# Attention and two feed-forward layers on one core: the features' positive part moves to ScalarE, three small operations move to GpSimd, and two buffers and twelve filler transposes change

## The chip, the cores and the metric

The kernel runs on one core of one Trainium2 chip. A core has five engines with a queue each: TensorE (PE in the profile; its weight loads are PEld), VectorE (DVE), ScalarE (ACT), GpSimd (POOL) and SyncE (SP, which here only issues DMAs). The metric is the device time in microseconds of one execution; a kernel's time is the median of its runs.

## The reference, cut to what matters

Three layers follow each other. The first is causal attention with a compressive memory, for 4 batches x 8 heads of 576 rows and 64 features; the second a feed-forward layer with squared ReLU (512 to 2048 to 512, for 2304 tokens); the third a layer of 8 experts of which each token takes one. The change touches the first two.

```python
scores = scale * q @ k.T                      # causal, softmax over keys
local  = softmax(scores) @ v
phi(x) = where(x > 0, x, exp(x) - 1) + 1      # = min(exp(x), 1) + max(x, 0)
mem    = (phi(q) @ M_prev) / (phi(q) @ z_prev + 1e-6)
x      = g * mem + (1 - g) * local            # g = sigmoid(beta), per head
x      = square(relu(x @ w_in)) @ w_out       # w_in, w_out are float64 in the input
x      = gate * relu(x @ w1[e]) @ w2[e]       # e = the best of 8 experts
```

## The kernel before, in words

**Precision.** Each large product is made of three: an operand a is split into a high part (a rounded to a shorter format) and a low part (a minus the high part), and high x high, high x low and low x high are added up in PSUM. So each operand costs a copy (mostly ACT) and a subtraction (DVE or POOL).

**Attention.** Two heads of a batch make a pair; there are 16 pairs, and each pair has 9 units (one for the last 64 rows of both heads, eight for 128 rows of one head). A loop (L627 to L693) takes one unit per step t (144 units, some 160 steps with the run-in and the run-out), and each step issues a bit of many strands: the scores of unit t (`ps`, L485), DVE's masked copy with its row minimum (`A<-ps`, `nm`, L489), ACT's exponential (L495), DVE's sum and reciprocal (`sm`, L503, L504), POOL's scaling (in the first four pairs a diagonal matrix `x_6` of 128x128, L443, afterwards the whole `A`, L446), TensorE's transposes of `A` (`pt`, L451 and L453), ACT's copies of them (`AT`, `ATa`, `ATb`, L641), and the product with the values (`xo`, L586). A page's name x with a line of attention is one of the tiles x_0 to x_8 that later hold the layer's output and until then serve as room.

**The features.** `prep(p)` prepares pair p while pair p-1 is worked on. PE transposes the keys (`tk`) and queries (`tq`); ACT copies them to `hk` and `hq` (L329, L335), DVE makes their low parts; ten DMAs from SP's queue (`moves`, L324) lay them out as `ks`, `qs` and `qz`. Then phi(q): ACT takes e = exp(q) (L355), DVE takes e = min(e, 1) (L359) and e = max(q, 0) + e (L360), POOL multiplies by z (`u`, L364), DVE sums u, adds, and inverts (`nr`, L394 to L398), POOL multiplies e by it (L402), and PE transposes e into `pT`, the memory's operand (L409 to L416). `hq` and `u` share one buffer (tag "hu").

**Conversion.** In the same loop the first half of the 64-bit weights is converted, 16 pieces of 512 columns. A piece has six small steps, and a loop step takes one of them: ACT takes the high words' absolute value (L142); DVE clamps them (L144) and shifts them (L145); DVE merges the sign (L147); DVE merges the low word (L149), which frees the raw buffer for the next DMA; ACT rounds to the high part (L152); POOL subtracts for the low part (L154). The second half is converted later, after attention, in the same way but for its last step.

**The feed-forward layer** begins at loop step 46 (pair 5). Its first chunk's input is split pair by pair by `split_part`: ACT makes `xh` (L733), DVE `xl` (L734). From there on a loop step also holds 12 matmuls of layer 1 (L776) or 6 of layer 2 (L815 to L817).

**What sets the order.** `later(d, engine, f)` puts f into step t + d. Up to step 8 DVE, POOL and SP run in the order of the code, DVE and POOL up to step 71; ACT is free from step 9 on, DVE and POOL from step 72 on. Where an engine is free, a scheduler places its instructions, except that each softmax operation stays behind the instruction recorded before it (`pinned`). PE's order is that of the code throughout. `BUSY` names the early steps at whose start `busy` issues that many transposes of the identity into a PSUM bank that nobody reads (L624).

Of the kernel before, what the change touches and what calls it, by code (L numbers as in the profile page):

```python
# [9 lines left out]
F32 = DT.float32  # L10
F32R = DT.float32r
BF16 = DT.bfloat16
I32 = DT.int32
AF = mybir.ActivationFunctionType
ALU = mybir.AluOpType
# [9 lines left out]
NPP = H // 2  # L25
# [18 lines left out]
W_LEAST = as_float(896 << 20)  # L44
# [12 lines left out]
START, EARLY, MIX = (3, 2, 1), 5, 1  # L57

FREE = 72
STRICT, BUSY = 9, {-5: 14, 0: 12, 2: 6, 4: 4}  # L60


TURN0, TURN1 = 5, 3
# [55 lines left out]
def conversion(nc, st, sh, half, n, lo_eng, w_in, w_out, queue=None, put=nullcontext):  # L119

    V = nc.vector
    raw = st.tile([128, 512, 2], I32, name="raw", tag="raw")
    f = n // 2
    f0 = half * 1024 + f * 128
    queue = queue or nc.sync
    if n % 2 == 0:
        queue.dma_start(raw.rearrange("p (c f) w -> p c (f w)", c=4),
                        w_in[:, f0:f0 + 128].bitcast(I32).rearrange("(c p) f -> p c f", p=128))
    else:
        queue.dma_start(raw.rearrange("p f w -> p (f w)"), w_out[f0:f0 + 128].bitcast(I32))  # L130
    sl = slice((f % 2) * 512, (f % 2) * 512 + 512)
    j = f // 2 + 4 * (n % 2)
    hi, lo = sh.Wh[half][j][:, sl], sh.Wl[half][j][:, sl]
    top, low = raw[:, :, 1], raw[:, :, 0]
    yield
    if half == 0 and n % 4 < 2:
        t = sh.x1[NCH - 4].rearrange("p a b -> p (a b)").bitcast(I32)[:, n % 4 * 512:n % 4 * 512 + 512]
    else:
        t = st.tile([128, 512], I32, name="wt", tag="wt", bufs=WT)
    tf = t.bitcast(F32)  # L140
    with put():
        nc.scalar.activation(tf, top.bitcast(F32), AF.Abs)  # L142
    yield
    V.tensor_scalar(tf, tf, W_LEAST, W_MOST, ALU.max, ALU.min)  # L144
    V.tensor_scalar(t, t, 3, 0x3FFFFFFF, ALU.logical_shift_left, ALU.bitwise_and)  # L145
    yield
    V.scalar_tensor_tensor(t, top, -0x40000000, t, ALU.bitwise_and, ALU.bitwise_or)  # L147
    yield
    V.scalar_tensor_tensor(t, low, 29, t, ALU.logical_shift_right, ALU.bitwise_or)  # L149
    yield  # L150
    with put():
        nc.scalar.copy(hi, tf)  # L152
    yield
    lo_eng.tensor_tensor(lo, tf, hi.bitcast(F32), ALU.subtract)  # L154
    yield
# [36 lines left out]
def attention(tc, sh, q, k, v, M, z, beta, w_in, w_out, mlp, step):  # L192

    nc = tc.nc
    with ExitStack() as ctx:
# [41 lines left out]
        def later(d, eng, f):  # L237
            queue.setdefault((now[0] + d, eng), []).append(f)
# [68 lines left out]
        def prep(p):  # L307
# [5 lines left out]
            if p == 0:  # L313
                hk = qs.rearrange("p a b -> p (a b)")[:, :S]
                hq, lq = ks[:, 0], ks[:, 1]
            else:
                hk = st.tile([128, S], F32R, name="hk", tag="hk", bufs=1)
                hq = st.tile([128, 512], F32R, name="hq", tag="hu", bufs=1)
                lq = st.tile([128, 512], F32R, name="lq", tag="lq", bufs=1)
            qz = new_qz(p) if p else None  # L320
            state[p] = (qs, ks, hq, lq, hk, kl, vn, Mt, qz)
# [30 lines left out]
            u = st.tile([128, 5, 128], F32, name="u", tag="hu", bufs=1)  # L352
            nr = st.tile([128, 10], F32, name="nr", tag="nr")

            later(1, "act", lambda: nc.scalar.activation(e, qn, AF.Exp))  # L355
            yield

            def phi():
                nc.vector.tensor_scalar_min(e, e, 1.0)  # L359
                nc.vector.scalar_tensor_tensor(e, qn, 0.0, e, ALU.max, ALU.add)  # L360

            def weigh():
                later(1, "dve", phi)
                later(1, "pool", lambda: nc.gpsimd.tensor_tensor(u, e, zb.unsqueeze(1).to_broadcast([128, 5, 128]), ALU.mult))  # L364

            if p:
                weigh()
# [332 lines left out]
class Mlp:  # L700
# [23 lines left out]
    def split_part(self, kc):  # L724
# [6 lines left out]
        xl.append(b)  # L731
        x = sh.x1[0][:, kc]
        self.later(2, "act", lambda: nc.scalar.copy(a, x))  # L733
        self.later(2, "dve", lambda: nc.vector.tensor_tensor(b, x, a.bitcast(F32), ALU.subtract))  # L734

    def split_chunk(self, hf, cc):
        if (hf, cc) == (1, NCH - 1):
# [822 lines left out]
```

## Time and profile before

| | us |
|---|---|
| median of 3 runs | 944.61 |
| lowest and highest run | 941.22 and 950.59 |
| the profiled execution's own time | 942.87 |
| its span, from first to last instruction | 941.1 |

| engine | busy us | share of the span |
|---|---|---|
| PE | 898.7 | 95% |
| PEld | 787.7 | 84% |
| DVE | 597.2 | 63% |
| ACT | 524.0 | 56% |
| POOL | 298.4 | 32% |

Read the table as an average over stages: attention alone fills about the first 106 us, attention beside the feed-forward layer the time to about 365 us, then come the rest of the feed-forward layer and the experts. TensorE's granted clock is 0.985 of full speed on average over the span.

### The profile page before, as it was taken

The numbers are of one execution on the slowest core, as the hardware profiler recorded it, in microseconds if no ns is written. First come the engines' busy times: TensorE is split into PE (matmuls) and PEld (weight loads), VectorE is DVE, ScalarE is ACT, GpSimd is POOL, SyncE is SP. The second block draws the span as 40 slices with busy tenths as digits, with TensorE's granted clock in tenths as the row PEclk, the third lists the DMA queues.
The fourth block names the chain that finished last, engine by engine and source line by source line (L and its number), as shares of the span: only waits on it lengthen the run. The fifth ranks groups of instructions, "written<-read, shape, count | busy, mean of one in ns | idle before, by whom it ended". The sixth has DMA issues, their size and how long they took to land.

```text
span 941.1 us, 19239 instructions
## 1 busy us (share of the span) xinstructions
PE 898.7 (95%) x6307; PEld 787.7 (84%) x6307; DVE 597.2 (63%) x1743; ACT 524.0 (56%) x1367; POOL 298.4 (32%) x356
## 2 busy tenths in 40 slices
PE   7978799899999999999999999999999999999993
PEld 5866678788888888898898888888899999999882
DVE  4688977756565653798357778889653535353651
ACT  4677878786676765777555555665322424242540
POOL 5366656744444442000211112442312211111111
PEclk9799999999999999999999999999999999999997
DMA  6666667644444410454201115221061625252521
GB/s 171 144 148 172 177 149 194 159 117 118 110 113 109 103 33 24 137 171 142 92 23 46 46 46 184 76 68 56 24 225 45 208 85 185 86 191 85 184 63 36
DMA packets 107657, 106.86 MB, mean 114 GB/s; under 512 B 66159, under 2 KB 76399, under 8 KB 107520
## 3 DMA queue, kind: packets, MB, share of 16 engines
q1 hardware_dynamic: 101104, 90.17, 34.0%
q0 software_dynamic: 4544, 13.67, 4.5%
q8 instruction: 66, 1.08, 0.5%
q10 hardware_dynamic: 1872, 1.34, 0.5%
q14 instruction: 71, 0.58, 0.2%
HBM read 71.32 MB, written 15.22 MB: 92 GB/s over the span
## 4 chain that ended last, share of the span: by engine, by line
PE 80%; DVE 8%; issue 5%; ACT 2%; DMA 2%; POOL 1%; SPq 0%; ACTq 0%; POOLq 0%; DVEq 0%
PE ps L776 20%; PE psh L1355 11%; PE y L815 7%; PE y L817 7%; PE y L816 7%; PE xo L586 5%; PE ps L485 4%; PE psy L1373 4%; PE psy L1371 4%; PE psy L1372 3%; PE pt L451 3%; DVE A L489 2%; PE pt L453 1%; DVE x L925 1%; PE xo L555 1%
## 5 line engine op out<-in xcount | busy, mean ns | idle before, releaser
L489 DVE CUSTOM_DVE_ANT_0 A<-ps,mask 128x256 f32<-128x256 f32 (+4 forms) x160 | 75.2, 477 | 80.9 <-PE ps L485 79.8
L776 PE MATMUL ps<-xh,Wh 128*128 128x256 f32 x416 | 120.8, 290 | 0.0
L446 POOL TENSOR_SCALAR A<-A,sm,g 128x512 f32<-128x512 f32 (+4 forms) x108 | 86.8, 811 | 102.3 <-DVE sm L504 44.3
L776 PE MATMUL ps<-xl,Wh 128*128 128x256 f32 x416 | 117.6, 283 | 0.0
L776 PE MATMUL ps<-xh,Wl 128*128 128x256 f32 x416 | 117.4, 282 | 0.0
L815 PE MATMUL y<-Wh,gh 128*128 128x512 f32 x288 | 115.6, 402 | 0.0
L817 PE MATMUL y<-Wh,gl 128*128 128x512 f32 x288 | 113.4, 394 | 0.1
L816 PE MATMUL y<-Wl,gh 128*128 128x512 f32 x288 | 113.3, 393 | 0.0
L495 ACT ACTIVATE A<-A,nm 128x576 f32<-128x576 f32 (+2 forms) x144 | 85.0, 590 | 48.4 <-DVE nm L489 21.4
L1357 ACT ACTIVATE hh<-psh 128x512 fp32r<-128x512 f32 x44 | 26.3, 598 | 145.9 <-PE psh L1355 84.8
L780 ACT ACTIVATE r<-ps 128x256 f32<-128x256 f32 x144 | 54.8, 380 | 85.9 <-PE ps L776 77.6
L1355 PE MATMUL psh<-xTh,Wh 128*128 128x256 f32 x352 | 100.0, 284 | 0.9 <-PEq L1363 0.7
L1355 PE MATMUL psh<-xTh,Wl 128*128 128x256 f32 x352 | 99.5, 283 | 0.2 <-DVE Wl L116 0.2
L1355 PE MATMUL psh<-xTl,Wh 128*128 128x256 f32 x352 | 99.3, 282 | 0.0
L786 DVE TENSOR_TENSOR gl<-r,gh 128x256 fp32r<-128x256 f32 x144 | 67.9, 472 | 36.2 <-ACT gh L785 35.8
L1358 DVE SCALAR_TENSOR_TENSOR hl<-psh,hh 128x512 fp32r<-128x512 f32 x44 | 30.4, 690 | 94.0 <-ACTq L1345 38.1
L776 PEld LDWEIGHTS ps<-xh,Wh 128*128 128x128 f32 x416 | 79.1, 190 | 3.9 <-issue 0.4
L776 PEld LDWEIGHTS ps<-xl,Wh 128*128 128x128 f32 x416 | 79.2, 190 | 2.8 <-issue 0.2
L776 PEld LDWEIGHTS ps<-xh,Wl 128*128 128x128 f32 x416 | 79.3, 191 | 0.0
L785 ACT CAST gh<-r 128x256 fp32r<-128x256 f32 x144 | 58.6, 407 | 34.6 <-PE y L816 31.9
L1355 PEld LDWEIGHTS psh<-xTh,Wh 128*128 128x128 f32 x352 | 66.9, 190 | 2.5 <-ACTq L1345 1.1
L1355 PEld LDWEIGHTS psh<-xTl,Wh 128*128 128x128 f32 x352 | 66.8, 190 | 0.8
(349 smaller groups left out, 2414.6 us busy)
## 6 DMA issues: line engine op xcount, KB each, us to landing
x<-in_moe_w_dram SPq DMA_DIRECT2D x48, 512.0 KB, 4.1
ks<-hk SPq DMA_DIRECT2D x60, 128.0 KB, 3.3
raw<-in_moe_w_in_dram SPq DMA_DIRECT2D x15, 512.0 KB, 3.8
raw<-in_moe_w_out_dram SPq DMA_DIRECT2D x15, 512.0 KB, 4.2
x2p<-x SPq DMA_DIRECT2D x18, 256.0 KB, 2.3
x2d<-x SPq DMA_DIRECT2D x18, 256.0 KB, 2.0
vn<-in_v_dram SPq DMA_DIRECT2D x32, 128.0 KB, 2.8
part<-x2p SPq DMA_DIRECT2D x16, 256.0 KB, 3.0
```

The costliest lines, as they stand in the source:

```text
L446: nc.gpsimd.tensor_scalar(A, A, a, b, ALU.mult, ALU.mult)
L489: nc.vector.tensor_tensor_reduce(A[:, a:a + w], tiles[j][:, :w], mask[:, end - w:end], -1.0, 3e38, ALU.add, ALU.min, nm[:, j:j + 1])
L495: nc.scalar.activation(A[:, :n], A[:, :n], AF.Exp, bias=nm[:, 0:1], scale=-1.0, accum_out=sm[:, i:i + 1])
L586: nc.tensor.matmul(x[hs, cols], vn[:, kb, hs], mov, start=h is None and kb == 0, stop=h is not None and end and kb == last)
L776: nc.tensor.matmul(ps[:, :CH], a, b, start=n == 0, stop=n == len(ops) - 1)
L780: self.later(1, "act", lambda: nc.scalar.activation(r, ps[:, :CH], AF.Relu))
L785: self.later(3, "act", lambda: nc.scalar.copy(gh, r))
L786: self.later(3, "dve", lambda: nc.vector.tensor_tensor(gl, r, gh.bitcast(F32), ALU.subtract))
L815: nc.tensor.matmul(y, gh[:, sl], wh, start=first, stop=False)
L816: nc.tensor.matmul(y, gh[:, sl], wl, start=False, stop=False)
L817: nc.tensor.matmul(y, gl[:, sl], wh, start=False, stop=last)
L1355: nc.tensor.matmul(ps[:, a], w[kc][:, sl], x[:, kc], start=kc + j == 0, stop=kc + j == 5)
```

## The change

Six edits. (1) `BUSY` gets two more steps: 8 filler transposes at step 5 and 4 at step 6. (2) The clamp of the conversion (L144) goes to POOL for the first half of the weights, in a step of its own; the shift that shared its step goes to the next one, beside the sign's merge, so a piece has as many steps as before. (3) `hq` of pairs 1 to 6 gets a buffer of its own, in the ring of two that the feed-forward layer uses for its output `x2`; from pair 7 on it shares "hu" with `u` as before. (4) ACT takes u = max(q, 0) behind e = exp(q), and DVE makes e = min(e, 1) + u in one instruction in place of two. (5) z's product, which overwrites u, comes one loop step later from pair 3 on. (6) `xl` of the first chunk goes from DVE to POOL.

```diff
-STRICT, BUSY = 9, {-5: 14, 0: 12, 2: 6, 4: 4}
+STRICT, BUSY = 9, {-5: 14, 0: 12, 2: 6, 4: 4, 5: 8, 6: 4}
...
     with put():
         nc.scalar.activation(tf, top.bitcast(F32), AF.Abs)
     yield
-    V.tensor_scalar(tf, tf, W_LEAST, W_MOST, ALU.max, ALU.min)
+    (nc.gpsimd if half == 0 else V).tensor_scalar(tf, tf, W_LEAST, W_MOST, ALU.max, ALU.min)
+    yield
     V.tensor_scalar(t, t, 3, 0x3FFFFFFF, ALU.logical_shift_left, ALU.bitwise_and)
-    yield
     V.scalar_tensor_tensor(t, top, -0x40000000, t, ALU.bitwise_and, ALU.bitwise_or)
...
                 hk = st.tile([128, S], F32R, name="hk", tag="hk", bufs=1)
-                hq = st.tile([128, 512], F32R, name="hq", tag="hu", bufs=1)
+                if p < NPP + 3:
+                    hq = mlp.st.tile([128, 512], F32R, name="hq", tag="x2")
+                else:
+                    hq = st.tile([128, 512], F32R, name="hq", tag="hu", bufs=1)
...
-            later(1, "act", lambda: nc.scalar.activation(e, qn, AF.Exp))
+            def grow():
+                nc.scalar.activation(e, qn, AF.Exp)
+                nc.scalar.activation(u, qn, AF.Relu)
+
+            later(1, "act", grow)
             yield
 
             def phi():
-                nc.vector.tensor_scalar_min(e, e, 1.0)
-                nc.vector.scalar_tensor_tensor(e, qn, 0.0, e, ALU.max, ALU.add)
+                nc.vector.scalar_tensor_tensor(e, e, 1.0, u, ALU.min, ALU.add)
 
             def weigh():
                 later(1, "dve", phi)
-                later(1, "pool", lambda: nc.gpsimd.tensor_tensor(u, e, zb.unsqueeze(1).to_broadcast([128, 5, 128]), ALU.mult))
+                later(2 if p > 2 else 1, "pool", lambda: nc.gpsimd.tensor_tensor(u, e, zb.unsqueeze(1).to_broadcast([128, 5, 128]), ALU.mult))
...
         x = sh.x1[0][:, kc]
         self.later(2, "act", lambda: nc.scalar.copy(a, x))
-        self.later(2, "dve", lambda: nc.vector.tensor_tensor(b, x, a.bitcast(F32), ALU.subtract))
+        self.later(2, "pool", lambda: nc.gpsimd.tensor_tensor(b, x, a.bitcast(F32), ALU.subtract))
```

Line numbers of the changed kernel are larger by 1 to 6 behind the edits (L364 is L370 there, L443 is L449, L485 is L491, L624 is L630).

How the instructions stand on three engines, before and with the change. First PE at loop steps 5 and 6 (`w` is the fillers' bank, `tp` the transposed features, `pt` the transposed softmax); before:

```order
L485 MATMUL ps<-kl,ks 128x256
L485 MATMUL ps<-qs,ks 128x384 x2
L485 MATMUL ps<-kl,ks 128x384
L409 MATMUL tp<-ident,e 128x128 x4
L453 MATMUL pt<-x_6_96,A_144 128x128 x4
L453 MATMUL pt_377<-x_6_96,A_144 128x128
L453 MATMUL pt<-x_6_96,A 128x128 x4
```

With the change:

```order
L491 MATMUL ps<-kl,ks 128x256
L630 MATMUL w<-ident 128x128 x8
L491 MATMUL ps<-qs,ks 128x384 x2
L491 MATMUL ps<-kl,ks 128x384
L415 MATMUL tp<-ident,e 128x128 x4
L459 MATMUL pt<-x_6_96,A_144 128x128 x4
L459 MATMUL pt_386<-x_6_96,A_144 128x128
L630 MATMUL w<-ident 128x128 x4
L459 MATMUL pt<-x_6_96,A 128x128 x4
```

Two rows of fillers came in; the rest of PE's order, to the program's end, is the same.

Second, POOL in pair 1 (L364, with the change L370, is z's product for pair 2; L144 is a clamp, L154 a conversion's last step); before:

```order
L402 TENSOR_TENSOR e<-e,nr 128x640
L443 TENSOR_SCALAR x_6_96<-ident,sm,g_186 128x128 x4
L364 TENSOR_TENSOR u<-e,zb 128x640
L443 TENSOR_SCALAR x_6_96<-ident,sm,g_186 128x128 x2
L154 TENSOR_TENSOR Wl_0_79<-x_5_95,Wh_0_71 128x512
```

With the change:

```order
L408 TENSOR_TENSOR e<-e,nr 128x640
L144 TENSOR_SCALAR x_5_95<-x_5_95 128x512
L449 TENSOR_SCALAR x_6_96<-ident,sm,g_186 128x128 x4
L370 TENSOR_TENSOR u<-e,zb 128x640
L144 TENSOR_SCALAR x_5_95<-x_5_95 128x512
L449 TENSOR_SCALAR x_6_96<-ident,sm,g_186 128x128 x2
L154 TENSOR_TENSOR Wl_0_79<-x_5_95,Wh_0_71 128x512
```

Two clamps came in, one of them between z's product and the next two scalings. In the following pairs an `xl` (L740) comes in as well, behind two scalings.

Third, ACT in pair 4, where the features of pair 5 are made (`AT` are the transposed softmax of the last 64 rows); before:

```order
L355 ACTIVATE e<-qn 128x640
L495 ACTIVATE A,sm<-A,nm 128x128
L142 ACTIVATE wt<-raw 128x512
L641 COPY AT<-pt 128x512
L641 COPY AT_1435<-pt_1433 128x128
L495 ACTIVATE A,sm<-A,nm 128x384
```

With the change:

```order
L359 ACTIVATE e<-qn 128x640
L501 ACTIVATE A,sm<-A,nm 128x128
L360 ACTIVATE u<-qn 128x640
L142 ACTIVATE wt<-raw 128x512
L647 COPY AT<-pt 128x512
L647 COPY AT_1450<-pt_1448 128x128
L501 ACTIVATE A,sm<-A,nm 128x384
```

The positive part (L360) came in ahead of the high words' absolute value and of the copies that TensorE waits for; in other pairs the scheduler puts it elsewhere in the same stretch.

## Rows read from the trace of the kernel before

**Rows 1.** Two stretches: busy us (instructions) of PE, PEld, DVE, ACT, POOL, clock, DMA, GB/s.

```profile
40.00:190.00 150.00, 130.72 (x1051) 107.82 (x1052) 123.29 (x371) 119.16 (x343) 93.40 (x99) 0.99 0.67 168
190.00:370.00 180.00, 180.00 (x1420) 155.56 (x1419) 103.98 (x380) 124.88 (x377) 75.41 (x88) 1.00 0.39 93
```

**Rows 2.** TensorE's waits between 34 and 190 us, first and last of 15.

```profile
PE ps L485 <- DVE nm L489: 4.0, 5, 1.3
...
PE pt L451 <- DVE kl L330: 0.2, 1, 0.2
```

**Rows 3.** Short stretches, columns as in the first group.

```profile
15.20:21.30 6.10, 2.87 (x18) 2.19 (x18) 3.87 (x17) 3.83 (x13) 2.75 (x6) 1.00 0.73 235
22.90:33.00 10.10, 10.10 (x60) 8.63 (x58) 4.83 (x20) 4.47 (x15) 3.04 (x3) 0.50 0.75 168
...
91.00:99.30 8.30, 4.87 (x30) 3.44 (x30) 7.52 (x24) 8.22 (x24) 4.59 (x6) 1.00 0.55 158
177.80:183.50 5.70, 2.64 (x18) 2.04 (x18) 5.70 (x20) 3.71 (x11) 3.59 (x3) 0.97 0.53 119
183.50:186.70 3.20, 3.20 (x14) 3.01 (x15) 1.22 (x4) 1.65 (x5) 3.09 (x6) 0.52 0.76 170
```

**Rows 4.** TensorE in order of time: start, us, instruction [idle before and releaser].

```profile
10.52 0.88 PE L624 MATMUL w<-ident 128*128 128x128 f32 x6
...
16.54 0.61 PE L485 MATMUL ps<-qs,ks 64*128 64x384 f32 x2 [1.38 <-DVE nm L489]
...
20.33 0.49 PE L453 MATMUL pt<-x,A 128*128 128x128 f32 x2 [1.38 <-ACT AT L641]
21.26 1.13 PE L453 MATMUL pt<-x,A 128*128 128x128 f32 x8 [0.45 <-POOL x L443]
```

**Rows 5.** DVE's groups by form up to 380 us: busy us, mean ns, idle before.

```profile
L359 DVE TENSOR_SCALAR e<-e 128x640 f32<-128x640 f32 x16 | 8.7, 544 | 2.4 <-ACT e L355 2.4
L144 DVE TENSOR_SCALAR x<-x 128x512 f32<-128x512 f32 x8 | 4.1, 509 | 1.4 <-ACT x L142 1.3
L144 DVE TENSOR_SCALAR wt<-wt 128x512 f32<-128x512 f32 x8 | 3.3, 412 | 0.0
L734 DVE TENSOR_TENSOR xl<-x,xh 128x256 fp32r<-128x256 f32 x4 | 1.8, 440 | 0.0
```

**Rows 6.** All engines in order of time, pair 2's features.

```profile
45.36 0.82 DVE L360 SCALAR_TENSOR_TENSOR e<-qn,e 128x640 f32<-128x640 f32 x1
...
45.40 0.60 SPq L324 DMA_DIRECT2D qz<-hq  x1
...
48.09 1.55 POOL L364 TENSOR_TENSOR u<-e,zb 128x640 f32<-128x640 f32 x1 [5.53 <-DVE sm L503]
...
48.13 2.06 DVE L147 SCALAR_TENSOR_TENSOR x<-raw,x 128x512 int32<-128x512 int32 x1
...
50.57 0.94 PE L453 MATMUL pt<-x,A 128*128 128x128 f32 x6 [1.33 <-POOL x L443]
```

**Rows 7.** POOL's groups by form: busy us, mean ns, idle before.

```profile
L446 POOL TENSOR_SCALAR A<-A,sm,g 128x512 f32<-128x512 f32 x24 | 24.7, 1038 | 27.4 <-ACT pT L410 12.9 <-DVE sm L504 10.7 <-ACT ATb L641 2.5
...
L754 POOL TENSOR_TENSOR xl<-x,xh 128x256 fp32r<-128x256 f32 x16 | 12.0, 778 | 57.2 <-ACT xh L753 57.2
```

**Rows 8.** ACT's exponential of the queries, by form: busy us, mean ns, idle before.

```profile
L355 ACT ACTIVATE e<-qn 128x640 f32<-128x640 f32 x14 | 10.5, 752 | 0.0
```

**Rows 9.** TensorE in order of time, pair 4.

```profile
96.85 1.12 PE L555 MATMUL xo<-pT,Mt 128*128 128x512 f32 x2 [1.36 <-ACT pT L416]
...
99.22 0.63 PE L451 MATMUL pt<-ident,A 128*128 128x128 f32 x4 [0.48 <-ACT AT L641]
```

**Rows 10.** All engines in order of time, pair 8's features.

```profile
168.12 0.60 SPq L324 DMA_DIRECT2D qz<-hq  x1
...
171.49 0.68 ACT L142 ACTIVATE wt<-raw 128x512 f32<-128x512 f32 x1
...
172.69 1.96 POOL L364 TENSOR_TENSOR u<-e,zb 128x640 f32<-128x640 f32 x1 [0.96 <-DMA kn<-in_k_dram]
```

## The prediction, made before the changed kernel ran

> **What bounds the kernel now.** I read the busy time by stretch first, then TensorE's waits, then the clock. From 190 us on TensorE is the bound without a gap: it is busy 180.00 of 180 us while ACT is busy 124.88, DVE 103.98 and POOL 75.41 [rows 1]. All six edits lie in attention and in the conversion beside it, that is before about 365 us, so behind 190 us they can cost only what TensorE's full queue does not cover. What is left to win lies before 190 us. From 40 to 190 us TensorE is busy 130.72 of 150 us and idles 19.3, while DVE is busy 123.29 and ACT 119.16 [rows 1]: the three form a ring (scores, row minimum, exponential, transposes, copies, scores again), and none is full all the time. Who ends TensorE's waits there is told by 15 rows that come to 19.4 us, of which the first and the last stand here [rows 2]: ACT ends nine of them, 10.9 us, DVE four, 6.0, POOL two, 2.5.
>
> The second thing to see is the clock. Between 22.9 and 33.0 us the granted clock is 0.50, that is 1.2 GHz in place of 2.4, and TensorE is busy all 10.10 us while ACT is busy 4.47 and DVE 4.83 [rows 3]: here TensorE alone is the bound, and only since it is slow. In the 6.1 us before the fall it was busy 2.87, with gaps of 1.38, 1.38 and 0.45 us [rows 3, 4]. A second fall, to 0.52 over 3.2 us from 183.5, follows a stretch with 2.64 of 5.7 us busy; a stretch with 4.87 of 8.3 us busy (91.0 to 99.3) is followed by none [rows 3].
>
> **The change, part by part.** The sum is made against the profiled execution, 942.87 us, which is 1.7 below the median of 944.61 and inside the 941.22 to 950.59 of the runs.
>
> *Fillers.* Six of them took 0.88 us [rows 4], so eight take about 1.2 and four 0.6. Eight stand in front of the scores that came after the gap of 1.38 and four in front of the transposes that came after the gap of 0.45; the second gap of 1.38 stays open. In the first gap they cost nothing, in the gap of 0.45 at most 0.15; I take 0.1. They raise the busy time before the fall from 2.87 to about 4.5 of 6.1 us (1.2 and 0.4 more), 73%, above the 59% (4.87 of 8.3) after which the clock held. So I take it that the clock holds. Then TensorE's work of 10.1 us needs 5.05, and ACT's 4.47 plus a positive part of 0.75 [rows 8], 5.2, is the next bound: at most 4.9 us are won, at least none (it falls all the same). Since ACT reached only 79% in the ring (119.16 of 150), 5.2 becomes 6.6, and I take 3.5.
>
> *DVE's relief.* Gone from DVE before 190 us are nine of the sixteen min instructions (9 x 0.544 = 4.9), the sixteen clamps (4.1 + 3.3) and four `xl` (1.8) [rows 5], together 14.1 us. The surviving instruction of phi has the form of the one that stays today, two tensors in, and I keep its 0.82 [rows 6]. The shift, moved one step back, no longer stands ahead of the next row minimum. What can arrive at once is what DVE ends of TensorE's waits, 6.0; the lower bound is nothing, where ACT's turn stands right behind. I take half, 3.0, since ACT ends nearly twice as much as DVE. Behind 190 us the rest of the min instructions is worth nothing.
>
> *The buffer.* In pair 2 DVE had finished phi at 46.2, but POOL's product began at 48.09, when the DMA of `qz` from `hq`, issued at 45.40, had landed: u and hq are one buffer [rows 6]. Behind the product stood the scalings, and TensorE waited 1.33 us for one. With a buffer of its own, hq no longer holds u, the product can run at 46.2, and that wait goes. Bounds: nothing, or POOL's whole 2.5; I take 1.3. The ring of `x2` that lends the buffer is not in use by the feed-forward layer until its first chunk is done, by which time hq has only pair 6 left there; I cost that at nothing. Were it not so, a query copy on ACT would stand behind the landing of an `x2` store. On SP two issues of raw weights change places with one of the moves, at no cost.
>
> *POOL's load.* Nearest rows: a two-step operation on 128x512 took 1.038 on POOL, a subtraction of 128x256 0.778 [rows 7]. Sixteen clamps and four `xl` are 16.6 + 3.1 = 19.7 us more on POOL, which idles 56.6 of the 150 us [rows 1]. A clamp makes a new wait: DVE's shift, and all of DVE's order behind it up to step 71, needs it a step later. A step before pair 5 lasts about 2 us (the feed-forward layer begins at step 46, at 106 us), and where z's product and a clamp fall into one step they take 2.6; so the shift may be late by 0.6, once in each of pairs 1 to 8, 4.8 at most, nothing where the product starts earlier as above. I take 0.5.
>
> One thing weighs against this part. In pair 2 DVE's sign merge, of 512 columns, lasted 2.06 us, from the start of POOL's product to 0.55 us behind its end; the phi instruction of the same form, of 640 columns, had taken 0.82 [rows 6]. So about 1.2 us of DVE were lost beside one product of 1.55. The Trainium skill (SBUF — State Buffer, section "SBUF: two separate sides") says that VectorE and GpSimd take a shared pair of ports as an exclusive lock for a whole instruction, where VectorE reads two tensors from SBUF or runs in a two-port mode; by it a clamp on GpSimd is no free move, and this term would be up to 5.6 slower in place of 3.0 faster; the row agrees as far as one pair can. By the row alone, POOL's new 19.7 us cost DVE between nothing and 19.7; DVE is rid of 14.1, so the sum of both lies between -14.1 and +5.6. I take the relief as above, and the other end is a rival.
>
> *ACT's load.* The positive part reads and writes what the exponential does, 0.75 us [rows 8]. In pair 4 ACT is the bound: busy 8.22 of 8.30 us [rows 3], and TensorE waits 1.36 for `pT` and 0.48 for `AT` [rows 9]; with the change the positive part stands ahead of `AT`. If it arrives in full in each of pairs 2 to 6 it costs 3.8, if nowhere nothing; I take two of the five, 1.5. At the very start it stands ahead of the casts that the first scores need, 0.75 late, against 0.54 that DVE saves there: I take 0.3. Behind 190 us TensorE's queue covers it; without that cover seven pairs would cost 5.3.
>
> Sum: 942.87 + 0.1 - 3.5 - 3.0 - 1.3 + 0.5 + 1.5 + 0.3 = 937.5 us, 0.8% below the median.
>
> **The rivals.** *Forecast* (0.50): as above, 932 to 941.
>
> *DVE is master everywhere* (0.18): ACT's exponentials are late only since the row minima are. Then DVE's 6.0, POOL's 2.5 and the clock's 4.9 arrive in full, the second fall goes as well (half of 3.2, 1.6), and the positive part hides: 942.87 - 15.0 = 928, range 924 to 932. For it: DVE busy 5.70 of 5.70 us before the second fall [rows 3]. Against it: pair 4 [rows 9].
>
> *The clock falls all the same* (0.18), since one gap of 1.38 stays and the positive part adds a delay before it: 937.5 + 3.5 = 941, range 938 to 944.
>
> *POOL takes back what DVE gave* (0.08). Each of POOL's new instructions holds DVE up for its length, as the product did with the sign merge. The place is the conversion, where the clamp runs while DVE merges another piece, and the end is DVE's net +5.6 in the ring in place of -3.0: 937.5 + 8.6 = 946, slower than before. It decides from the point where DVE loses more than 14.1 us to POOL. Beside it stands the lock of the Trainium skill's page named above, which would give this result if every one of them met such an instruction. Against it: many of DVE's instructions here read one tensor from PSUM and a mask, and the product that held DVE longest moves ahead.
>
> *ACT waits for a DMA* (0.06). From pair 7 on the positive part writes the buffer that hq's DMAs still read. In pair 8 the last one was issued at 168.12 and the product that waited for it began at 172.69; ACT's place for the positive part is behind the instruction that ends at 172.17 [rows 10]. So ACT would stand 0.5 us and then work 0.75, and all copies out of PSUM with it. Nine pairs x 1.25 = 11 us, if TensorE's queue covers none of it: 937.5 + 11 = 948.5. Against it: ACT is busy 124.88 of 180 us [rows 1].
>
> **How the numbers follow.** The prediction is the forecast's 937.5. The range leaves out the slow two rivals (0.14) and the low tail of the fast one: 928 to 945. The forecast's own range is 932 to 941. What a measurement of this kernel can tell from no change is about 1%: 935.2 to 954.1 around 944.61. Faster by more: the fast rival (0.18) and, of the forecast, the part below 935.2 (0.22), 0.40. Slower by more: the upper tails of the last two and what I have not thought of, 0.06. Within: 0.54.
>
> **What would show it.** Clock 1.00 from 15 to 40 us, and the scores of pair 1 some 3 us earlier; if the clock falls at a later place before 60 us, the first term failed. The product of pair 2 within 1 us of phi, and no wait of TensorE for the scaling behind it. Clamps on POOL of about 1 us, DVE's shift without a wait for them. TensorE's waits between 34 and 190 us: DVE's near 3, ACT's unchanged or larger, with `AT` of pair 4 later against the scores by up to 0.75. Wrong I would be if DVE's mean times of the merges rise by more than their sixteen clamps saved, or if TensorE idles behind 190 us.

## The result, and the profile after

The changed kernel takes 954.34 us (median of 6 runs, 953.09 to 957.32), the kernel before, run beside it, 945.32 (941.22 to 950.59). The ratio is 1.0114, with an interval of 1.0083 to 1.0145: slower, by 9.0 us between these medians and by 10.8 by the ratio, where 937.5 (928 to 945) was forecast. The profiled execution of the changed kernel took 953.85 us, its span is 952.1.

The windows of the changed kernel answer to [rows 1, 3]; the columns are the same.

```profile
22.90:33.00 10.10, 9.77 (x85) 8.08 (x84) 6.21 (x26) 7.96 (x24) 4.39 (x6) 1.00 0.73 166
40.00:190.00 150.00, 127.50 (x1007) 103.80 (x1006) 105.87 (x311) 114.56 (x324) 113.87 (x107) 0.97 0.65 157
190.00:370.00 180.00, 177.17 (x1365) 153.00 (x1365) 105.81 (x385) 128.79 (x381) 74.06 (x93) 0.98 0.41 98
190.00:200.00 10.00, 7.17 (x33) 6.16 (x34) 6.96 (x25) 5.69 (x15) 5.84 (x8) 0.66 0.58 128
```

The clock now holds from 22.9 to 33 us (1.00, before 0.50). But from 40 to 190 us VectorE (DVE) is busy 17.4 us less than before and TensorE 3.2 less: what VectorE was relieved of turned into idle time, not into speed. GpSimd (POOL) is busy 20.5 us more. And the stretch from 190 us, full before, has a hole: 7.17 of 10 us at a clock of 0.66.

Where the time goes is told by the first scores of each pair (the first matmul of 128x320 into `ps` from `qbh`). Their starts, against the kernel before (30.21 us in pair 1, 104.83 in pair 5, 156.33 in pair 7, 202.96 in pair 9); behind pair 9's first scores the difference stays as it is. Each row is one profiled execution beside one of the kernel before, so 2 or 3 us in a place can be chance (clamp_back stands at +3.01 in pair 9, and its ratio is 1.0000); the medians are from different chips, so small differences go by the ratios, each to the kernel before run beside it:

```
kernel (median us; ratio to before, 95%)            pair 1  pair 5  pair 7  pair 9
the change (954.3; 1.0083 to 1.0145)                 -2.10   +1.42   +5.36  +11.30
clamp_back (944.6; 0.9980 to 1.0019)                 -2.42   -1.44   -0.64   +3.01
clamp_alone (958.6; 1.0102 to 1.0179)                +0.10   +7.18  +11.92  +16.23
relu_undone (956.7; 1.0099 to 1.0168)                -2.96   +2.22   +6.22  +10.38
fillers_alone (940.9; 0.9953 to 0.9995)              -3.13   -3.20   -1.67   -3.07
clamp_and_relu_undone (940.1; 0.9956 to 0.9996)      -3.09   -2.40   -2.57   -3.99
fillers_and_relu (952.7; 1.0065 to 1.0126)           -2.79   +5.81   +7.44  +10.36
multiply_for_clamp (943.2; 0.9976 to 1.0015)         -2.14   -1.51   -2.59   +1.04
shift_behind (952.5; 1.0059 to 1.0138)               -2.63   -0.87   +2.91   +9.64
load_only (943.8; 0.9999 to 1.0035)                  -2.89   -2.75   -1.79   -0.22
relu_to_pair_6 (943.0; 0.9977 to 1.0009)             -2.12   -2.73   -0.48   -1.50
vector_less (935.3; 0.9890 to 0.9936)                -3.14   -3.22   -5.80   -9.11
clamp_earlier (945.4; 1.0000 to 1.0044)              -2.64   -0.56   -1.99   +1.77
bunch_alone (944.2; 0.9979 to 1.0030)                -2.39   +0.19   -0.52   +3.42
best_candidate (942.5; 0.9964 to 0.9999)             -3.46   -0.39   -1.71   -0.87
behind_and_earlier (947.3; 1.0037 to 1.0071)         -2.58   -3.30   -3.16   +2.13
behind_xl_on_vector (953.5; 1.0097 to 1.0130)        -2.61   +0.03   +1.93   +9.15
subtract_load (946.7; 1.0017 to 1.0061)              -2.51   -1.75   +1.03   +2.06
```

GpSimd's groups by form, from 15 to 215 us of the changed kernel (busy us, mean ns), beside [rows 7]; L144 is the clamp, L452 the multiplication that was L446:

```profile
L144 POOL TENSOR_SCALAR x<-x 128x512 f32<-128x512 f32 x8 | 15.4, 1919 | 0.2 <-ACT x L142 0.2
L144 POOL TENSOR_SCALAR wt<-wt 128x512 f32<-128x512 f32 x8 | 15.3, 1914 | 0.0
...
L452 POOL TENSOR_SCALAR A<-A,sm,g 128x512 f32<-128x512 f32 x10 | 10.1, 1020 | 7.0 <-DVE sm L510 6.9
```

A clamp takes 1.92 us, not the 1.04 that the prediction took from the multiplication of the same shape. VectorE's waits from 20 to 205 us (total us, times, longest):

```profile
DVE wt L146 <- POOL wt L144: 6.7, 4, 2.4
DVE e L366 <- ACT u L360: 5.4, 4, 2.5
DVE x L146 <- POOL x L144: 4.2, 5, 1.1
```

The shift (L146) waits 10.9 us for clamps, phi (L366) 5.4 for the Relu. How one such wait reaches TensorE stands in the order of time, pair 8:

```profile
186.91 1.91 POOL L144 TENSOR_SCALAR wt<-wt 128x512 f32<-128x512 f32 x1
...
188.79 1.26 POOL L154 TENSOR_TENSOR Wl<-wt,Wh 128x512 fp32r<-128x512 f32 x1
188.85 1.48 DVE L146 TENSOR_SCALAR wt<-wt 128x512 int32<-128x512 int32 x1 [2.37 <-POOL wt L144]
...
190.33 0.48 DVE L495 CUSTOM_DVE_ANT_0 A<-ps,mask 128x320 f32<-128x320 f32 x1
...
190.87 0.61 PE L491 MATMUL ps<-ks,qs 128*128 128x512 f32 x1 [2.77 <-DVE nm L495]
```

VectorE stands 2.37 us for the clamp. Then its shift lasts 1.48 us beside GpSimd's next subtraction, which started 0.06 us before it. That is so throughout: of the changed kernel's 16 shifts, the twelve beside a scaling of one tensor on GpSimd took 0.41 to 0.48 us; the four that began beside an instruction with two tensors took 0.91 to 1.50, and each ended 0.28 us after that instruction. The row minimum comes behind wait and shift, TensorE waits 2.77 us for it, and its clock falls (the window at 190 us).

### The profile page after: what moved, and what is told of

Read it like the earlier page. It is cut to its first block, busy times and chain, and to the rows that moved or that the text cites. A ratio compares the mean times of both kernels' runs of the same rounds, so it can differ in the third digit from the quotient of the medians.

```text
span 952.1 us, 19216 instructions
## 1 busy us (share of the span) xinstructions
PE 901.7 (95%) x6319; PEld 787.9 (83%) x6319; DVE 585.3 (61%) x1707; ACT 533.8 (56%) x1383; POOL 323.8 (34%) x376
## 4 chain that ended last, share of the span: by engine, by line
PE 74%; DVE 10%; issue 6%; POOL 5%; ACT 2%; DMA 2%; SPq 0%; ACTq 0%; POOLq 0%; DVEq 0%
PE ps L782 19%; PE psh L1361 11%; PE y L821 7%; PE y L823 6%; PE y L822 6%; PE xo L592 4%; PE psy L1379 3%; PE psy L1377 3%; PE ps L491 3%; PE psy L1378 3%; PE pt L457 3%; DVE A L495 2%; DVE x L931 1%; POOL wt L144 1%; POOL x L144 1%
## 5 line engine op out<-in xcount | busy, mean ns | idle before, releaser
L452 POOL TENSOR_SCALAR A<-A,sm,g 128x512 f32<-128x512 f32 (+4 forms) x108 | 78.2, 732 | 87.8 <-DVE sm L510 31.2
L1377 PE MATMUL psy<-Wh,hh 128*128 128x512 f32 x168 | 67.0, 399 | 0.1
```

The source lines that it names most:

```text
L452: nc.gpsimd.tensor_scalar(A, A, a, b, ALU.mult, ALU.mult)
L1377: nc.tensor.matmul(y[h], xh, wh, start=g + a == 0, stop=False)
```

## The experiments

Theory W was that the loss is the wait: a slow clamp ahead of VectorE's shift, with the softmax's minima behind the shift. Theory R was that ScalarE's (ACT's) Relu costs it. Others came up on the way. (Two operations move to GpSimd, the clamp and `xl`, and one tile, `hq`, gets another buffer; the title counts more.)

**clamp_back, clamp_alone, relu_undone, fillers_alone: which part?** The first is the change with the clamp as before:

```diff
-    (nc.gpsimd if half == 0 else V).tensor_scalar(tf, tf, W_LEAST, W_MOST, ALU.max, ALU.min)
-    yield
+    V.tensor_scalar(tf, tf, W_LEAST, W_MOST, ALU.max, ALU.min)
     V.tensor_scalar(t, t, 3, 0x3FFFFFFF, ALU.logical_shift_left, ALU.bitwise_and)
+    yield
```

> The changed kernel with one part undone: the clamp is VectorE's again, in one step with its shift as before; the other five edits stay. Theory W (the wait: a clamp of 1.91 us on GpSimd, 16 of them, stands ahead of VectorE's shift, and all that lies behind the shift in VectorE's order is late): the 10.9 us of waits of the shift go, the scores of pairs 1 to 9 come earlier by 10 to 13 us in all, 941 to 944 us. Theory R (ScalarE's Relu: 16 x 0.74 us more on ScalarE, and phi waits 5.4 us for it): the loss stays, 950 to 954 us.

clamp_alone is the opposite diff on the kernel before.

> The kernel before with one part of the change done: the clamp of the first weights' conversion on GpSimd in a step of its own, the shift a step later. Theory W: 952 to 958 us (945.3 and the 10 us that pairs 5 to 8 lost, and falls of the clock that differ from place to place). Theory R: 944 to 947 us, as the kernel before.

relu_undone:

```diff
-                nc.scalar.activation(u, qn, AF.Relu)
...
-                nc.vector.scalar_tensor_tensor(e, e, 1.0, u, ALU.min, ALU.add)
+                nc.vector.tensor_scalar_min(e, e, 1.0)
+                nc.vector.scalar_tensor_tensor(e, qn, 0.0, e, ALU.max, ALU.add)
```

> The changed kernel with the Relu undone: VectorE computes phi in two instructions, ScalarE only the exponential. Theory W: 951 to 955 us, since the wait of phi for ScalarE (9.3 us in 9 waits) lies mostly beside the wait of the shift. Theory R: 943 to 947 us.

fillers_alone is the kernel before with `5: 8, 6: 4` in `BUSY`.

> The kernel before with the added fillers alone (two entries of the table BUSY). If the fillers keep the clock up through pair 0 and nothing takes it back: granted clock 1.00 from 22.9 to 33 us, the scores of pair 1 some 3 us earlier and the whole at 941 to 943 us. The rival, that the 3 us are given back in pair 1 where the clock falls after the next gap (in the changed kernel it was 0.83 from 40 to 50 us): 944 to 946 us.

Measured: 944.6, 958.6, 956.7 and 940.9 us. The clamp makes the loss (the first three lie 0.6, 0.6 and 1.7 us above theory W's ranges, and far from theory R's): without it the rest of the change is at the kernel before, alone it costs 1.4% (1.0 to 1.8), and undoing the Relu gives nothing back while the clamp is there. The fillers hold the clock, and nothing takes the 3 us back (fillers_alone's window):

```profile
22.90:33.00 10.10, 9.62 (x88) 8.24 (x87) 7.41 (x30) 7.56 (x24) 4.86 (x7) 1.00 0.70 159
```

**clamp_and_relu_undone, fillers_and_relu, relu_to_pair_6: what the Relu costs.** The first joins the diffs of clamp_back and relu_undone.

> The changed kernel without its clamp on GpSimd and without its Relu: what is left is the fillers, hq's buffer, the later product of z and the low part xl on GpSimd. The fillers alone gave 940.9, the change with the clamp undone 944.6. If the Relu is what costs these 3.7 us (phi waits for it 7.3 us in 4 waits with the clamp undone): 939 to 942 us. If hq's buffer, the product or xl cost them: 943 to 946 us.

The second is fillers_alone with the Relu and the one instruction of phi, but hq still in u's buffer:

```diff
-            later(1, "act", lambda: nc.scalar.activation(e, qn, AF.Exp))
+            later(1, "act", grow)
...
```

> The kernel before with two parts of the change: the fillers and the Relu. If the Relu costs the 3.7 us: 943.5 to 946 us, with the loss in pairs 7 and 8 (the scores of pair 9 against the kernel before at +2 to +3 us, where the fillers alone stood at -3.1). If not: 940 to 942 us.

The third is clamp_back with the Relu only where hq has a buffer of its own:

```diff
+                if p < NPP + 3:
+                    nc.scalar.activation(u, qn, AF.Relu)
...
```

> The changed kernel with the clamp back on VectorE, and ScalarE's Relu in pairs 0 to 6 alone, where hq has the buffer that it doesn't share with u; pairs 7 to 15 have phi in VectorE's two instructions again. Theory S (the Relu waits, on ScalarE, for hq to leave the buffer that it shares with u from pair 7 on; with the clamp back pairs 7 and 8 lost 3.65 us against the kernel before): pair 9's scores at -0.5 us or earlier against the kernel before instead of +3.0, 940 to 942 us. Theory R (16 x 0.74 us more on ScalarE is what costs): 942.5 to 945 us.

Measured: 940.1, 952.7 and 943.0 us. The second came out far beyond what I had expected: with a shared buffer the Relu has to stand behind hq's transfers, and so late in ScalarE's order (its own waits for them are 1.3 us in two), and phi on VectorE waits for it, 28.2 us in nine waits:

```profile
DVE e L363 <- ACT u L357: 28.2, 9, 6.6
```

So, by these waits, hq's own buffer is what makes the Relu affordable (the product's later step and `xl` on GpSimd, which this run lacks as well, were not tried one by one). From pair 7 on, where the change goes back to the shared one, the same wait of phi returns. In clamp_back the Relu stands 3.9 us behind the exponential in pair 7, and in pair 8 it waits for a transfer:

```profile
144.21 0.78 ACT L359 ACTIVATE e<-qn 128x640 f32<-128x640 f32 x1
...
148.07 0.73 ACT L360 ACTIVATE u<-qn 128x640 f32<-128x640 f32 x1
...
148.91 0.82 DVE L366 SCALAR_TENSOR_TENSOR e<-e,u 128x640 f32<-128x640 f32 x1 [1.92 <-ACT u L360]
...
173.44 0.74 ACT L360 ACTIVATE u<-qn 128x640 f32<-128x640 f32 x1 [0.88 <-DMA kn<-in_k_dram]
...
174.28 0.82 DVE L366 SCALAR_TENSOR_TENSOR e<-e,u 128x640 f32<-128x640 f32 x1 [3.78 <-ACT u L360]
```

and phi waits for it 1.92 us in pair 7 and 3.78 in pair 8. Without the Relu from pair 7 on (relu_to_pair_6) VectorE has no such wait from 135 to 205 us, and pair 9 stands at -1.50 in place of +3.01. In the whole time that is 944.6 against 943.0 (ratios 1.0000 and 0.9993), within the spread of either, so the place is shown and the size is not; 943.0 itself lies where theory R had it. A second part is the start: the first scores come at 8.30 us in clamp_and_relu_undone, at 9.05 in clamp_back, 9.34 in relu_to_pair_6.

**multiply_for_clamp and clamp_forms: what the price hangs on.** The clamp is left out; other operations stand at its place on GpSimd (for the first half of the weights). In multiply_for_clamp:

```diff
+        nc.gpsimd.tensor_scalar(tf, tf, 1.0, 1.0, ALU.mult, ALU.mult)
```

> The changed kernel with the first weights' clamp left out: in its place GpSimd multiplies the same tile in place twice by 1.0, so order, steps, waits and shapes are the changed kernel's. If the price of 1.91 us belongs to the maximum and minimum: about 1.04 us each, as the softmax's multiplication of 128x512; by theory W the waits of the shift then fall from 10.9 us to under 5 and the time to 945 to 949 us. If it belongs to the place (in place, the tile, the company of VectorE's shifts): 1.9 us each and 953 to 956 us.

In clamp_forms, by the piece's number n:

```diff
+    elif n % 4 == 0:
+        nc.gpsimd.tensor_scalar(tf, tf, W_LEAST, None, ALU.max)
+    elif n % 4 == 1:
+        nc.gpsimd.tensor_scalar(tf, tf, W_LEAST, 1.0, ALU.max, ALU.mult)
+    elif n % 4 == 2:
+        nc.gpsimd.tensor_scalar(tf, tf, 1.0, 0.0, ALU.mult, ALU.add)
+    else:
+        nc.gpsimd.tensor_scalar(tf, tf, 1.0, W_MOST, ALU.mult, ALU.min)
```

> The changed kernel with four other operations at the clamp's place on GpSimd, in turn by n modulo 4, each leaving out a part of the clamp: the maximum alone, maximum then a multiplication by 1, a multiplication and an addition, a multiplication and the minimum. Max and min together took 1.91 us, two multiplications 0.62 us. If each of maximum and minimum has the high price by itself: about 1.0 to 1.3 us for the maximum alone and for the mixed pairs, 0.62 us for multiplication and addition. If one of them already brings a slow routine: 1.9 us wherever one stands.

The rows of GpSimd by form, of multiply_for_clamp (one of its two) and then of clamp_forms (L147 maximum alone, L149 maximum and multiplication, L151 multiplication and addition, L153 multiplication and minimum):

```profile
L145 POOL TENSOR_SCALAR wt<-wt 128x512 f32<-128x512 f32 x8 | 4.9, 615 | 0.0
```

```profile
L153 POOL TENSOR_SCALAR wt<-wt 128x512 f32<-128x512 f32 x4 | 7.7, 1935 | 0.3
L149 POOL TENSOR_SCALAR x<-x 128x512 f32<-128x512 f32 x4 | 7.7, 1928 | 0.2 <-ACT x L142 0.2
L147 POOL TENSOR_SCALAR x<-x 128x512 f32<-128x512 f32 x4 | 6.0, 1501 | 0.0
...
L151 POOL TENSOR_SCALAR wt<-wt 128x512 f32<-128x512 f32 x4 | 2.5, 620 | 0.0
```

The price is the operation's, and neither expectation had it whole: 0.62 us for multiplications and additions by constants, 1.50 for one maximum, 1.93 for any pair with a maximum or minimum in it. With 0.62 us in the clamp's place, and the order of instructions on TensorE, VectorE, ScalarE and GpSimd that of the change, the shift's waits are 2.4 us in place of 10.9 and the time is 943.2 (from 20 to 205 us):

```profile
DVE wt L149 <- POOL wt L145: 2.4, 3, 1.1
```

The length of the clamp alone makes the 11 us. clamp_forms, run once, took 950.5. The Trainium skill (GPSIMD Engine Reference, section "Engine selection") says that with one input GpSimd runs roughly at line rate; that fits 0.62 us beside VectorE's 0.41 to 0.51 [rows 5], and not the 1.92 of maximum and minimum, and the measurement decides.

**load_only, shift_behind, clamp_earlier: wait or load?** load_only is clamp_back with GpSimd's work and no wait; the order on the other engines is clamp_back's:

```diff
+        spare = sh.Wl[0][7][:, 512:1024]
...
+        nc.gpsimd.tensor_scalar(spare, spare.bitcast(F32), W_LEAST, W_MOST, ALU.max, ALU.min)
```

> The changed kernel with the clamp back on VectorE and, at the place of each of the 16 clamps on GpSimd, the same maximum and minimum of 128x512 on a tile that nothing waits for. So GpSimd carries the changed kernel's load (16 x 1.9 us), and VectorE's shift waits for nothing there. Against 944.6 us with the clamp back and 954.3 us of the change: theory W (the wait of the shift does the harm) 944 to 947 us; theory L (GpSimd's load does it: scalings and low parts behind the clamp in GpSimd's order are late) 951 to 957 us.

shift_behind is the change with the shift and its merge one step later:

```diff
     yield
+    yield
     V.tensor_scalar(t, t, 3, 0x3FFFFFFF, ALU.logical_shift_left, ALU.bitwise_and)
     V.scalar_tensor_tensor(t, top, -0x40000000, t, ALU.bitwise_and, ALU.bitwise_or)
-    yield
```

> The changed kernel with the shift and its merge one step later, together with the second merge, so that VectorE does a row minimum or more of the softmax between the clamp's start and the shift; the number of steps is unchanged. Theory W (the wait does the harm): the shift's waits fall from 10.9 us to under 4, 945 to 949 us. Theory L (GpSimd's load does the harm: 30.7 us more, under which low parts, scalings and VectorE's own instructions get late or longer): 952 to 956 us.

clamp_earlier:

```diff
+    half or nc.gpsimd.tensor_scalar(tf, tf, W_LEAST, W_MOST, ALU.max, ALU.min)
     yield
-    (nc.gpsimd if half == 0 else V).tensor_scalar(tf, tf, W_LEAST, W_MOST, ALU.max, ALU.min)
+    half and V.tensor_scalar(tf, tf, W_LEAST, W_MOST, ALU.max, ALU.min)
     yield
```

> The changed kernel with GpSimd's clamp issued one step earlier, in the step of its absolute value; VectorE's order stays the changed kernel's (two small swaps apart), GpSimd's load too. Theory W (the wait of the shift and what lies behind it in VectorE's order): the shift's waits fall from 10.9 us to under 4 and the time to 944 to 948 us. Theory C (whatever comes of a conversion that has a clamp of 1.9 us in it: the chain of one conversion is longer, its later steps late, VectorE's merges beside other GpSimd work): 950 to 955 us, as with the shift behind (952.5), whose waits were gone as well.

load_only carries more than the change's load,

```profile
L149 POOL TENSOR_SCALAR Wl<-Wl 128x512 fp32r<-128x512 f32 x16 | 33.2, 2076 | 0.1
```

and takes 943.8 us: 33 us more on GpSimd cost nothing that can be measured (ratio 1.0017, 0.9999 to 1.0035; clamp_back 1.0000). Theory L, that GpSimd's load does the harm, falls for maximum and minimum. clamp_earlier takes 945.4; the shift's waits are 4.0 us (2.5 and 1.5):

```profile
DVE wt L146 <- POOL wt L142: 2.5, 3, 1.3
...
DVE x L146 <- POOL x L142: 1.5, 2, 1.1
```

That is theory W, and gives back about 9 of the 10 to 11 us. But shift_behind stayed at 952.5, where theory L had it, with only 1.6 us of waits. Three runs looked into it.

**bunch_alone, behind_and_earlier, behind_xl_on_vector.** All have the step structure of shift_behind. bunch_alone has its clamp on VectorE (`V.tensor_scalar` in the clamp's line).

> The control of the run with the shift one step later: shift and both merges in one step as there, but the clamp on VectorE, in the step that it had on GpSimd. If the bunch of three instructions (2.0 to 2.9 us in a row on VectorE, row minima behind it) did the harm there: 949 to 953 us. If not: 943 to 946 us, as the run with the clamp back (944.6).

behind_and_earlier has clamp_earlier's diff as well.

> The kernel with the shift one step later, its clamps on GpSimd one step earlier: VectorE's order is that of the shift behind (952.5 us), but the clamp is over a whole step before the shift begins. If the slow clamp does harm there by ending just as the shift begins, where GpSimd's next subtraction starts at the same moment and holds the shift (one shift of 2.69 us was seen there): 943 to 947 us. If the bunch of shift and merges beside GpSimd's load does it: 950 to 954 us.

behind_xl_on_vector undoes `xl`:

```diff
-        self.later(2, "pool", lambda: nc.gpsimd.tensor_tensor(b, x, a.bitcast(F32), ALU.subtract))
+        self.later(2, "dve", lambda: nc.vector.tensor_tensor(b, x, a.bitcast(F32), ALU.subtract))
```

> The kernel with the shift one step later, and the low parts xl of the first chunk on VectorE again. In the run with the shift behind TensorE waited 3.28 us for an xl that stood behind clamp, scaling and subtraction in GpSimd's order. If that wait is what was left: 948 to 950 us. If not: 951 to 954 us.

Measured: 944.2, 947.3 and 953.5 us. Neither the bunch nor `xl` does it; an earlier clamp does, for about half of what separates shift_behind from bunch_alone (5 of 8 us by the medians, 4 of 9 by the ratios). One place where a late clamp harms without a wait on the books is this, in shift_behind:

```profile
186.00 1.91 POOL L144 TENSOR_SCALAR wt<-wt 128x512 f32<-128x512 f32 x1
187.88 1.26 POOL L154 TENSOR_TENSOR Wl<-wt,Wh 128x512 fp32r<-128x512 f32 x1
...
187.95 2.69 DVE L147 TENSOR_SCALAR wt<-wt 128x512 int32<-128x512 int32 x1 [0.70 <-POOL wt L144]
...
189.10 1.25 POOL L408 TENSOR_TENSOR e<-e,nr 128x640 f32<-128x640 f32 x1
...
192.66 0.88 PE L457 MATMUL pt<-ident,A 128*128 128x128 f32 x3 [4.84 <-DVE kl L333]
```

The shift begins as the clamp ends; so does GpSimd's next instruction, and the shift lasts 2.69 us, until two GpSimd instructions with two tensors are over. TensorE then waits 4.84. The other 3 to 5 us of shift_behind are not settled.

**subtract_load: which GpSimd instructions hold VectorE?** load_only with another spare instruction:

```diff
-        nc.gpsimd.tensor_scalar(spare, spare.bitcast(F32), W_LEAST, W_MOST, ALU.max, ALU.min)
+        nc.gpsimd.tensor_tensor(spare, spare.bitcast(F32), spare.bitcast(F32), ALU.subtract)
```

> As load_only, but GpSimd's 16 spare instructions, that nothing waits for, are subtractions of two 128x512 tensors (1.35 us each) in place of maximum and minimum. In load_only VectorE's conversion instructions came to 48.0 us, with the clamp back to 45.0. If a GpSimd instruction with two tensors in holds VectorE and one with a single tensor doesn't: the conversion's instructions come to 53 us or more, and the time to 945 to 948 us. If neither holds it: 45 to 49 us, and 943 to 945 us.

946.7 us; VectorE's conversion instructions come to 49.7 (counted the same way, 47.7 in load_only and 43.7 in clamp_back), between the two expectations. The spread over all of VectorE tells more: I took each of its instructions from 20 to 215 us, subtracted the shortest of its form, and put the excess over 0.1 us to the GpSimd instruction that lay longest beside it. In load_only 2.8 us fall to the 33.2 us of maximum and minimum, in subtract_load 6.7 us to the 18.6 us of subtractions; in the kernel before, 15.1 of 19.8 us fall to the 48.8 us of GpSimd's two-tensor instructions, 4.0 to the 41.7 us of its scalings of `A`. The changed kernel's clamps get 0.7 us in 30.7. The split goes by what lay beside an instruction, so it shows company, not cause; the shifts that ended 0.28 us after a subtraction are the closer evidence. In the whole time subtract_load (1.0017 to 1.0061) and load_only (0.9999 to 1.0035) can't be told apart.

**vector_less: what is VectorE's time worth?** fillers_alone with the clamp and the second merge left out of the first weights' conversion:

```diff
+    if half:
         V.tensor_scalar(tf, tf, W_LEAST, W_MOST, ALU.max, ALU.min)
...
+    if half:
         V.scalar_tensor_tensor(t, low, 29, t, ALU.logical_shift_right, ALU.bitwise_or)
```

> The kernel before with the fillers, and less work on VectorE: the clamp and the second merge of the first weights' conversion are left out (32 instructions, about 20 us, most of them between 20 and 205 us). The fillers alone gave 940.9 us. If relief of VectorE is worth what the prediction took (3.0 us for 14.1): 936 to 937 us. If VectorE is master everywhere in that stretch (the rival): 921 to 925 us. If VectorE's work there is hidden: 940 to 942 us.

935.3 us against 940.9, 5.6 for the 21.5 us that these 32 instructions took in fillers_alone: 0.26 us for each. The windows of fillers_alone and of vector_less:

```profile
40.00:190.00 150.00, 130.48 (x1045) 108.05 (x1044) 128.24 (x371) 119.75 (x343) 92.05 (x97) 0.99 0.67 163
```

```profile
40.00:190.00 150.00, 136.87 (x1107) 113.11 (x1105) 108.68 (x350) 123.75 (x355) 88.73 (x98) 0.99 0.68 165
```

**best_candidate** is clamp_earlier without the Relu.

> The changed kernel without the Relu, and with GpSimd's clamp one step earlier. By theory W, with the load harmless (load_only 943.8) and 0.28 us gained for each us less on VectorE (as in the run with less on VectorE), it is 2 us below the change without clamp and Relu (940.1): 937 to 940 us. By theory C 946 to 950 us.

942.5 us, above the 937 to 940 expected: 4.8 us of the shift's waits are left, and the relief seems to pay for little more than these. Faster than the kernel before, by a quarter of a per cent, are fillers_alone and clamp_and_relu_undone, and each about as much as the other.

## Why the prediction was wrong

The step that failed is *POOL's load*, taken at +0.5 us. It had two prices. The clamp was priced from the nearest row by shape, a multiplication [rows 7], where the operation decides: 1.92 us in place of 1.04. The wait of VectorE's shift was priced as 0.6 us once in each of pairs 1 to 8, 4.8 at most. It was 10.9: in 13 of 16 cases the shift began within 0.1 us of the clamp's end, so a step later on VectorE was, as a rule, no later than the clamp on GpSimd. The term's measured size is +10 to +11 (954.3 against 944.6 with the clamp back, ratios 1.0114 and 1.0000), alone about +13; multiply_for_clamp takes it away by the first price (3 of 16 shifts then begin within 0.1 us of GpSimd's end), clamp_earlier nearly by the second. The "4.8 at most" was no bound: it came from the step's average length and from the price that was too low.

The other steps:
- *Fillers*, -3.5: right. Clock 1.00, pair 1 3.1 us earlier, and 0.26% of the whole (0.05 to 0.47), 2.5 us. By the prediction's own sign, a fall of the clock before 60 us, the term failed in the changed kernel: TensorE waited 2.73 us to 39.65, and the clock is 0.50 from 41.0 to 44.3. In fillers_alone and clamp_back it is 1.00 from 40 to 50, so this fall comes with the clamp.
- *DVE's relief*, -3.0 for 14.1 us: the rate was right (0.21 taken, 0.26 measured by vector_less), but in the changed kernel nothing of it is seen: the wait put in was larger than what the work taken out could free.
- *The buffer*, -1.3: the mechanism was right, the product runs right behind phi (46.62 after 45.71 + 0.83 us; before 48.09 [rows 6]). But TensorE's wait for the scaling, 1.33 us before, is still 0.98, since a clamp now stands between the two:

```profile
46.62 1.55 POOL L370 TENSOR_TENSOR u<-e,zb 128x640 f32<-128x640 f32 x1 [6.19 <-DVE e L366]
...
48.15 1.92 POOL L144 TENSOR_SCALAR x<-x 128x512 f32<-128x512 f32 x1
...
50.05 1.59 POOL L449 TENSOR_SCALAR x<-ident,sm,g 128x128 f32<-128x128 f32 x2
...
50.84 0.94 PE L459 MATMUL pt<-x,A 128*128 128x128 f32 x6 [0.98 <-POOL x L449]
```

In clamp_back and multiply_for_clamp that wait is gone; in fillers_alone, without the buffer, it is 1.46. The buffer's own gain can't be measured: clamp_and_relu_undone, which has it, stands at 940.1, fillers_alone at 940.9. The prediction missed its larger role, that without it the Relu would cost some 12 us (952.7 against 940.9, with the reserve made above).
- *ACT's load*, +1.5 and +0.3 at the start: with the clamp back, 944.6 against 940.1 gives 4.5 by the medians, the ratios (1.0000 and 0.9976) 2.3, with intervals that overlap (0.9980 to 1.0019, 0.9956 to 0.9996). The first scores come 1.2 us late (9.35 for 8.18), for 0.3 taken; pairs 7 and 8 are the second place, by the mechanism of the rival *ACT waits for a DMA*, which had it for nine pairs at 11 us. Behind pair 9's first scores it is hidden.

Without the clamp, too, the sum was too good. Leaving out the clamp's price and relief it comes to about 938.6, 4 us below its 942.87 (an estimate: 937.5 less 0.5, and 1.6 for the 7.4 of 14.1 us of relief that were the clamps); clamp_back shows no gain at all (0.9980 to 1.0019). ACT's load seems to have taken more than its 1.8, and how the rest divides is open. Of the prediction's two signs of being wrong one came, TensorE's idle time behind 190 us (2.83 of 180 us); the merges rose less (25.0 to 27.3 us) than the clamps had taken (7.4).

No rival reached 954. *ACT waits for a DMA* (948.5) lies nearest, but with the Relu undone the loss stays (956.7). *POOL takes back what DVE gave* (946) had the right sign, but its mechanism is refuted for the clamps: 33 us of maximum and minimum beside VectorE cost nothing in load_only. The lock that the Trainium skill describes (SBUF — State Buffer, section "SBUF: two separate sides") makes no difference between GpSimd's instructions by how many tensors they read. Here the trace agrees for those with two tensors, as in the rows of shift_behind (whether the shift, which reads one tensor, runs in the two-port mode that the page names, no run shows), and not for those with one: in load_only nine of the eleven merges of two tensors that ran beside the spare maximum and minimum took 0.67 to 0.69 us, against 0.63 at best. The measurement decides. *DVE is master everywhere* falls with vector_less: 21.5 us less gave 5.6. *The clock falls all the same* is false in pair 0, but new falls came with the new waits (0.83 from 40 to 50 us, 0.66 from 190 to 200).

Still open: the last 3 to 5 us of shift_behind, and the sizes of Relu, buffer, product and `xl` one by one, each below what these runs can tell apart.

## What to carry to other kernels

In this kernel, maximum and minimum moved to an idle engine cost nothing by their load, and all by their latency: ask when the next instruction on an engine with a fixed order needs the result, and what stands behind that one. Price an operation on GpSimd by a row with the same operation, not with the same shape; where no row has it, the range has to reach well beyond the nearest (here 1.92 us against 1.04). When a consumer stands a step behind, give the moved work one step more: issued one step earlier, the same clamp cost 1 to 2 us in place of 10 to 11.

## What the runs showed of the hardware

- On GpSimd, 128x512 in 32-bit floats in one instruction: two multiplications by constants, or a multiplication and an addition, 0.62 us; by scalars from a tile 1.02; one maximum 1.50; maximum and minimum, or either with a multiplication, 1.91 to 1.94 (2.08 on load_only's spare tile); on VectorE maximum and minimum took 0.41 to 0.51 [rows 5].
- GpSimd's instructions on two tensors lengthen VectorE's beside them (6.7 us for 18.6 of spare subtractions; shifts of 0.43 us to 1.48, 1.50 and 2.69, each ending about 0.28 us after GpSimd's instruction); those on one tensor hardly do (2.8 for 33.2).
- In the changed kernel TensorE's waits of 2.73, 2.44 and 2.77 us at full clock (to 39.65, 142.06 and 190.87 us) were each followed by a granted clock of 0.50 (41.0 to 44.3, 143.4 to 146.7, 191.2 to 197.9), so there a wait cost more than its length. It is no rule: in clamp_alone a wait of 2.44 us, to 149.77, was followed by none (1.00 from 146 to 160).
